# First unit of a fused attention and gated-FFN kernel: pair 0 by the hardware queue, key maxima from PSUM, turns ahead of scores

## The chip, the cores and the metric

The kernel runs on one core of one Trainium2 chip. The metric is the device time in microseconds (us) of one execution; lower is better. Executions of one kernel agree within about 0.8%, so differences of 1 us (0.4%) need several runs, and most experiments below were timed in five rounds against the kernel before on the same chip. PE is the matmul engine, DVE the vector engine, ACT the scalar engine, POOL the engine that issues the casting DMAs (the software queue), and SP the engine that issues the others (the hardware queue).

## The reference, cut to what matters

```python
# q, k, v: (4, 8, 768, 64); out: (3072, 512)
k_sum = k.reshape(B, H, 24, 32, D).max(axis=3)      # one key per block of 32: the maximum
v_sum = v.reshape(B, H, 24, 32, D).mean(axis=3)     # one value per block: the mean
# softmax over a band of +-15 positions and the 24 block keys together
a = softmax(concat([masked(q k^T / 8), q k_sum^T / 8 + log(32)]))
x = a @ concat([v, v_sum])                          # heads side by side: 512 wide
# gated FFN, 512 -> 1536 -> 512, on all 3072 rows
out = x + sigmoid(x @ w_res) * ((gelu(x @ w_gate) * (x @ w_val)) @ w_out)
```

The kernel cuts the work into eight units of half a sequence (384 rows). In a unit the eight heads are four pairs; a pair fills the 128 partitions of a transpose. A unit is: turn q and k (transpose), scores, exponential, attention, transpose of the output (`xp` to `xT`), gate and value matmuls in twelve output blocks (fo 0 to 11), and the second FFN matmul. The attention of unit n+1 is woven into the FFN of unit n, so only the attention of the first unit stands bare. That bare part, the prologue, is what the change works on.

## The kernel before

The parts that the change and the argument touch, with cuts marked:

```python
# PSUM: eight banks. mm has four buffers, s one of two banks, ao and t one bank each
MM, AO, TT, SS = (ps_mm, "mm"), (ps_o, "ao"), (ps_t, "t"), (ps_s, "s")
...
load_tokens(kt, k, 0, 0, S, 0, 4)          # all loads on POOL, float32 cast to bf16
select(ident[:], ALU.not_equal, 1.0, 0, -1, 1)
load_tokens(qa, q, 0, 0, TU, 0, 4)
load_tokens(kt, k, 0, 0, S, 4, 8)
load_tokens(qa, q, 0, 0, TU, 4, 8)
... # v in seven pieces, then the weights in column chunks, then q's second half
keep_warm(13, wp)                          # matmuls on zeros, nobody reads them
for hp in range(2):
    k_step(0, hp, *MM)
    q_step(qa, 0, 0, TU, hp, *MM)
... # mask and scores of pair 0, turns of pair 2, scores of pair 1, and so on
for c in range(3, NC + 1):                 # block means of v, a piece at a time
    vsum_sum(0, *MM, range(c, c + 1), vs)
    keep_warm(2 if c < NC else 1, wp)
vsum_out(0, vs, 0, 2, nc.vector.tensor_copy)
vsum_out(0, vs, 2, 8, nc.scalar.copy)
homes = (AO, TT, MM, MM)                   # PSUM of the attention outputs of the four pairs
for p in (0, 2):
    for hp in (p, p + 1):
        av_part(0, hp, st, *homes[hp], blocks=False)   # the band
    for hp in (p, p + 1):
        av_part(0, hp, st, blocks=True)                # the block values
        av_norm(hp, st)                                # two DVE operations
keep_warm(3)
...
for hp in range(NP):
    xt_step(0, hp, st, *(TT if hp % 2 else AO), nc.scalar.copy)   # PSUM of the transposes
    ... # gate and value matmuls of fo 0 and 1, a quarter of the depth at a time
```

The zero matmuls (`keep_warm`, 30 of them in the prologue) keep PE occupied. And the first transpose (pair 0) writes to the bank `AO`, which holds the attention output of pair 0: it may start when pair 0 has been normalised, which it needs anyway.

The softmax here doesn't subtract the row's maximum and nothing guards it: scores larger than these inputs give would overflow.

Of the kernel before, what the change touches and what calls it, by code (L numbers as in the profile page):

```python
# [15 lines left out]
def kernel(  # L16
# [86 lines left out]
    with tc.manual_schedule():  # L103
# [17 lines left out]
        def mask_consts():  # L121
            nc.vector.memset(maskt[:], 1.0)
            select(maskt[0:96], ALU.is_ge, 0.0, -1, -1, 1)
            select(maskt[0:96], ALU.is_ge, 0.0, 2 * WIN - 1, 1, -1)
            nc.vector.tensor_scalar(nmask[:], maskt[:], 30000.0, -30000.0, ALU.mult, ALU.add)

# [4 lines left out]
        nc.vector.memset(bmean[:], 1.0 / BLK)  # L131
        vext_consts(0)

        kt, qa, qb = token_tile(0, S, "k0"), token_tile(0, TU, "qa"), token_tile(TU, S, "qb")
        k_sb[0] = kt
        load_tokens(kt, k, 0, 0, S, 0, 4)
        select(ident[:], ALU.not_equal, 1.0, 0, -1, 1)
        load_tokens(qa, q, 0, 0, TU, 0, 4)
        load_tokens(kt, k, 0, 0, S, 4, 8)
        load_tokens(qa, q, 0, 0, TU, 4, 8)  # L140
        select(bias_t[96:128, :], ALU.is_ge, -30000.0, NB - 1, 0, -1)
        load_values(0, 0)
        mask_consts()
        kw_consts(0)
        load_values(0, 1)
        select(bmean[:], ALU.is_ge, 0.0, 32 * (NB + 94) - WIN, -32, 1)
        select(bmean[:], ALU.is_ge, 0.0, 31 + WIN - 32 * (NB + 94), 32, -1)
        for c in range(2, NC + 1):
            load_values(0, c)
        nc.vector.memset(vsum[0][96:128, :, D:D + 1], 1.0)  # L150
# [3 lines left out]
        for c in range(6):  # L154
            sl = slice(c * 256, (c + 1) * 256)
            nc.gpsimd.dma_start(out=w_gate[:, :, sl], in_=wg_src[:, :, sl])
            nc.gpsimd.dma_start(out=w_val[:, :, sl], in_=wv_src[:, :, sl])
        load_tokens(qb, q, 0, TU, S, 0, H)
# [55 lines left out]
        def q_step(src, b, lo, hi, hp, pool, tag):  # L214
            tp = turn_pair(src, hp, pool, tag)
            nc.scalar.copy(qT[b % 2][hp][:, lo:hi].rearrange("d (p j) -> d p j", j=tp.shape[2]), tp)
# [59 lines left out]
        def mask_step():  # L276
            s = ps_s.tile([128, 2, 512], F32, tag="s", name="s")
            for hh in range(2):
                nc.tensor.matmul(s[:, hh, 0:TU].rearrange("p (t q) -> p t q", t=HT), ident[:],
# [4 lines left out]
        def s_step(u, hp, st, s=None, two=None, masked=True):  # L284
            b, half = u // 2, u % 2
            first = s is not None
            if two:
# [129 lines left out]
        def values_step(u, fo):  # L417

            b = u // 2 + 1
            first = 8  # L420
            if u in (2, 4) and first - 3 <= fo < first + 1:
                block_sums(vT[b], fo - first + 3)
            if u in (1, 2, 4) and fo >= first:
# [11 lines left out]
                if i in (2, 3):  # L435
                    vsum_bc(nb, 2 * i - 4, 0, HT)
                    vsum_bc(nb, 2 * i - 3, 0, HT)
# [9 lines left out]
        wp = ps_o.tile([128, 512], F32, tag="ao", name="wp")  # L447
        keep_warm(13, wp)
        nc.scalar.activation(pre[:], bias_t[0:1, :], AF.Exp)
        for hp in range(2):  # L450
            k_step(0, hp, *MM)
            q_step(qa, 0, 0, TU, hp, *MM)
        s = mask_step()
        keep_warm(3, wp)
        s_step(0, 0, st, s)
        k_step(0, 2, *MM)
        q_step(qa, 0, 0, TU, 2, *MM)
        s = mask_step()
        s_step(0, 1, st, s)
        k_step(0, 3, *MM)  # L460
        q_step(qa, 0, 0, TU, 3, *MM)
        s = mask_step()
        s_step(0, 2, st, s)
        v_spread(0, 0, HT // 2, 0)
        v_spread(0, 0, HT // 2, 1)
        vs = vsum_sum(0, *MM, range(0, 3))
        keep_warm(2, wp)
        s = mask_step()
        s_step(0, 3, st, s)
        keep_warm(2, wp)  # L470
        for c in range(3, NC + 1):
            vsum_sum(0, *MM, range(c, c + 1), vs)
            keep_warm(2 if c < NC else 1, wp)
        vsum_out(0, vs, 0, 2, nc.vector.tensor_copy)
        vsum_out(0, vs, 2, 8, nc.scalar.copy)
        nc.scalar.activation(pre[:], bias_t[0:1, :], AF.Gelu)
        homes = (AO, TT, MM, MM)
        for p in (0, 2):
            for hp in (p, p + 1):
                av_part(0, hp, st, *homes[hp], blocks=False)  # L480
            for hp in (p, p + 1):
                av_part(0, hp, st, blocks=True)
                av_norm(hp, st)
        keep_warm(3)
# [7 lines left out]
        for u in range(NU):  # L492
# [17 lines left out]
            for fo in range(FO):  # L510
# [33 lines left out]
                if u == 0 and fo >= FO - 2:  # L544
                    for hp in range(2 * (fo - FO + 2), 2 * (fo - FO + 2) + 2):
                        q_step(qb, 0, TU, S, hp, *(TT if hp % 2 else AO))
# [108 lines left out]
```

## Time and profile before

| | |
|---|---|
| time, median of 3 runs | 265.32 us (264.82 to 265.44) |
| span of the profiled execution | 262.5 us |
| PE busy | 96% of the span |
| last block means of v that wait for a load | 18.17 us |
| first gate matmul | 23.24 us |
| gate matmuls without gaps | from 25.60 us |

The first lines of parts 1 and 2 of the page: busy time and share of each engine, and PE's busy tenths in 40 slices of the span with the granted clock.

```profile
PE 251.4 (96%) x2263; PEld 142.0 (54%) x2288; DVE 174.8 (67%) x414; ACT 133.2 (51%) x228; POOL 100.1 (38%) x136
...
PE   7799999999999999999899999999999999999994
...
PEclk9999999999999999999999999999999999999999
```

The reader sees that PE is short of work only in the first two slices of 6.6 us each. The chain of waits (the work that ended last, in order of time: start, length, what):

```profile
10.30 7.83 DMA vext<-in_v_dram
...
18.17 0.38 PE vs L254
18.55 0.43 PE wp L415 x2
18.98 0.32 PE vs L254
...
19.68 2.07 PE ao L328 x96
21.75 0.16 issue
21.91 0.59 PE wp L415 x2
22.51 0.18 PE xp L347 x3
```

The chain waits for v to land, then makes the block means (vs) with zero matmuls (wp) between them, the whole attention (ao), three more zero matmuls (the trace holds two of them), and the transposes (xp).

### The profile page before, as it was taken

The numbers are of one execution on the slowest core, as the hardware profiler recorded it, in microseconds if no ns is written. First come the engines' busy times: TensorE is split into PE (matmuls) and PEld (weight loads), VectorE is DVE, ScalarE is ACT, GpSimd is POOL, SyncE is SP. The second block draws the span as 40 slices with busy tenths as digits, with TensorE's granted clock in tenths as the row PEclk, the third lists the DMA queues.
The fourth block names the chain that finished last, engine by engine and source line by source line (L and its number), as shares of the span: only waits on it lengthen the run. The fifth ranks groups of instructions, "written<-read, shape, count | busy, mean of one in ns | idle before, by whom it ended". The sixth has DMA issues, their size and how long they took to land.

```text
span 262.5 us, 5776 instructions
## 1 busy us (share of the span) xinstructions
PE 251.4 (96%) x2263; PEld 142.0 (54%) x2288; DVE 174.8 (67%) x414; ACT 133.2 (51%) x228; POOL 100.1 (38%) x136
## 2 busy tenths in 40 slices
PE   7799999999999999999899999999999999999994
PEld 2536555556555565556455565455645565555543
DVE  3754862589385889877836799687739763674424
ACT  2745449557575535745274535734364536453310
POOL 7966642997799305998500200010000100020000
PEclk9999999999999999999999999999999999999999
DMA  5999999999999999999991785344002200130012
GB/s 78 175 168 196 197 205 192 144 153 191 106 117 121 205 147 109 147 174 194 136 72 32 175 151 96 16 104 125 0 4 75 93 0 2 30 124 13 1 40 82
DMA packets 113483, 28.83 MB, mean 110 GB/s; under 512 B 100400, under 2 KB 111280, under 8 KB 113456
## 3 DMA queue, kind: packets, MB, share of 16 engines
q0 software_dynamic: 86992, 19.41, 87.3%
q1 hardware_dynamic: 26464, 9.05, 18.1%
q8 instruction: 18, 0.29, 0.5%
q14 instruction: 9, 0.07, 0.1%
HBM read 32.51 MB, written 6.29 MB: 148 GB/s over the span
## 4 chain that ended last, share of the span: by engine, by line
PE 86%; DMA 6%; POOL 3%; issue 1%; DVE 1%; ACT 1%; POOLq 0%; DVEq 0%
PE f L398 23%; PE vv L364 21%; PE g L364 20%; PE r L382 8%; PE ao L328 4%; PE gv L508 3%; DMA vext<-in_v_dram 3%; DMA kW<-k_sb 3%; PE s L296 2%; POOL vext L99 2%; PE xp L347 1%; PE tp L185 1%; PE vs L254 1%; PE gv L364 1%; POOL k L90 1%
## 5 line engine op out<-in xcount | busy, mean ns | idle before, releaser
L364 PE MATMUL vv<-xT,w_val 128*128 128x384 bf16 x364 | 74.5, 326 | 0.0
L370 ACT ACTIVATE ge<-g 128x384 f32<-128x384 f32 x87 | 42.8, 492 | 59.5 <-PE g L364 33.9
L364 PE MATMUL g<-xT,w_gate 128*128 128x384 bf16 x348 | 71.3, 326 | 1.2 <-DVE gvT L371 1.2
L371 DVE TENSOR_TENSOR gvT<-ge,vv 128x384 bf16<-128x384 f32 x91 | 49.6, 551 | 27.9 <-PE vv L364 26.3
L398 PE MATMUL f<-w_out,gvT 128*128 128x512 bf16 (+2 forms) x298 | 66.6, 362 | 0.7
L364 PEld LDWEIGHTS <-w_val 128*128 128x128 bf16 x368 | 36.0, 98 | 24.5 <-issue 0.9
L364 PEld LDWEIGHTS <-w_gate 128*128 128x128 bf16 x352 | 33.8, 98 | 23.3 <-issue 1.8
L409 POOL DMA_DIRECT2D out_dram<-o x12 | 6.6, 546 | 98.8 <-DVE rz L336 83.9
L398 PEld LDWEIGHTS <-gvT 128*128 128x128 bf16 x312 | 28.3, 98 | 28.2
L388 ACT ACTIVATE th<-r 128x512 f32<-128x512 f32 x24 | 14.2, 602 | 25.8 <-PE r L382 25.8
L172 POOL DMA_DIRECT2D k_sb<-in_k_dram x24 | 20.1, 853 | 12.9 <-DMA w_out<-in_moe_w_out_dram 5.3
L403 DVE SCALAR_TENSOR_TENSOR th<-th,f 128x512 f32<-128x512 f32 (+2 forms) x26 | 16.7, 641 | 12.3 <-PE f L398 8.5
L382 PE MATMUL r<-w_res,xT 128*128 128x512 bf16 x88 | 23.7, 380 | 0.6 <-issue 0.3
L99 POOL DMA_DIRECT2D vext<-in_v_dram x28 | 23.2, 870 | 1.4 <-PE vv L364 0.8
L313 DVE TENSOR_TENSOR P<-P,maskt 128x768 bf16<-128x768 bf16 x28 | 15.5, 558 | 11.5 <-ACT P L305 7.5
L172 POOL DMA_DIRECT2D q_sb<-in_q_dram x24 | 19.7, 863 | 0.0
L338 DVE TENSOR_TENSOR xn<-ao,rz 128x384 bf16<-128x384 f32 x32 | 17.8, 557 | 1.1
L349 ACT COPY xT<-xp 128x384 bf16<-128x384 bf16 x20 | 9.3, 482 | 17.5 <-PE xp L347 17.5
L305 ACT ACTIVATE P<-s,bias_t 128x768 bf16<-128x768 f32 x18 | 16.3, 906 | 3.0 <-PE s L296 2.9
L405 DVE SCALAR_TENSOR_TENSOR o<-th,xn 128x512 f32<-128x512 f32 (+2 forms) x26 | 16.9, 651 | 0.9
L336 DVE RECIPROCAL rz<-ao 128x6 f32<-128x6 f32 x32 | 6.0, 189 | 13.1 <-PE ao L328 13.1
L302 ACT ACTIVATE P<-s,bias_t 128x384 bf16<-128x384 f32 x28 | 14.6, 578 | 0.0
(87 smaller groups left out, 247.2 us busy)
## 6 DMA issues: line engine op xcount, KB each, us to landing
out_dram<-o POOLq DMA_DIRECT2D x12, 256.0 KB, 2.8
out_dram<-o SPq DMA_DIRECT2D x11, 256.0 KB, 5.1
vext<-in_v_dram POOLq DMA_DIRECT2D x20, 128.0 KB, 7.3
k_sb<-in_k_dram POOLq DMA_DIRECT2D x24, 96.0 KB, 6.2
q_sb<-in_q_dram POOLq DMA_DIRECT2D x24, 96.0 KB, 4.1
w_gate<-in_moe_w_gate_dram POOLq DMA_DIRECT2D x6, 256.0 KB, 8.9
w_val<-in_moe_w_val_dram POOLq DMA_DIRECT2D x6, 256.0 KB, 9.1
w_out<-in_moe_w_out_dram POOLq DMA_DIRECT2D x3, 512.0 KB, 14.1
```

The source lines that it names most:

```text
L99: nc.gpsimd.dma_start(out=dst, in_=v[b, :, lo:hi, :].rearrange("h p d -> p h d"))
L172: nc.gpsimd.dma_start(out=sb[b][:, h // 2, :, h % 2 * D:h % 2 * D + D], in_=src[b, h].rearrange("(c p) d -> p c d", c=NC))
L305: nc.scalar.activation(P.rearrange("p a t q -> p a (t q)"), s[:, :, 0:TU], AF.Exp, scale=scale, bias=bias_t[:])
L313: nc.vector.tensor_mul(Pf, Pf, maskt.unsqueeze(1).to_broadcast([128, 2 * HT, QT]))
L338: nc.vector.tensor_mul(xn, ao[:, :, :, 0:D], rz.to_broadcast([128, NSUB, 2, D]))
L364: nc.tensor.matmul(acc[:, 0:TU], w[:, ko, fs], st["xT"][:, ko, :], start=(ko == 0), stop=(ko == KO - 1))
L370: nc.scalar.activation(ge[:], g[:, 0:TU], AF.Gelu)
L371: nc.vector.tensor_mul(gvT[:, fo, :], ge[:], vv[:, 0:TU])
L382: nc.tensor.matmul(r[:], st["xT"][:, ko, ss], w_res[:, ko, :], start=(ko == 0), stop=(ko == KO - 1))
L398: nc.tensor.matmul(st["f", sub][:, 0:c1 - c0], gvT[:, fo, ss], w_out[:, fo, c0:c1], start=(fo == 0), stop=(fo == FO - 1))
L403: nc.vector.scalar_tensor_tensor(th, th, 1.0, f[:, 0:c1 - c0], ALU.add, ALU.mult)
L405: nc.vector.scalar_tensor_tensor(o[:, 0:c1 - c0].rearrange("p (k d) -> p k d", d=128), th.rearrange("p (k d) -> p k d", d=128), 0.5, st["x ...
```

## The change

Its intent: start the first scores earlier, have the band part of the attention done before v has fully landed, and so reach the dense part sooner. Pair 0 of k and q comes by the hardware queue in float32 and is cast on ACT and DVE. The key maxima are reduced straight from the transposes in PSUM, and only for the half of the tiles that the first unit needs; the other half (`k_later`) is filled in amid the gate. Each pair's turns stand ahead of the scores of the pair before. q's second half is loaded ahead of the last weight chunk and turned behind fo 9.

```diff
-        load_tokens(kt, k, 0, 0, S, 0, 4)
+        nc.sync.dma_start(out=kf[:], in_=k[0, 0:2].rearrange("h (p j) d -> p h (j d)", j=8))
+        nc.sync.dma_start(out=qf[:], in_=q[0, 0:2, 0:TU].rearrange("h (p j) d -> p h (j d)", j=4))
+        load_tokens(kt, k, 0, 0, S, 2, 4)
         select(ident[:], ALU.not_equal, 1.0, 0, -1, 1)
-        load_tokens(qa, q, 0, 0, TU, 0, 4)
-        load_tokens(kt, k, 0, 0, S, 4, 8)
-        load_tokens(qa, q, 0, 0, TU, 4, 8)
+        load_tokens(qa, q, 0, 0, TU, 2, 4)
+        for h in (4, 6):
+            load_tokens(kt, k, 0, 0, S, h, h + 2)
+            load_tokens(qa, q, 0, 0, TU, h, h + 2)
+        select(maskt[0:96], ALU.is_ge, 0.0, -1, -1, 1)
+        select(maskt[0:96], ALU.is_ge, 0.0, 2 * WIN - 1, 1, -1)
+        load_values(0, 0)
... (cut: constants earlier; the block values of three later units moved to other output blocks; in the weight loop:)
+            if c == 5:
+                load_tokens(qb, q, 0, TU, S, 0, H)
... (cut: k_first, which copies a turned pair; its second half:)
+        def k_first_rest(tp, kw):
+            ks = work.tile([128, NB], BF16, tag="ks", name="ks")
+            nc.vector.tensor_reduce(out=ks[:], in_=tp.rearrange("d j (n w) -> d n j w", w=4),
+                                    axis=mybir.AxisListType.XY, op=ALU.max)
+            ... three copies for the first HT tiles; k_later makes the same three for the others
... (cut; the prologue, its end:)
-        keep_warm(13, wp)
+        keep_warm(8, s1[0])
...
-        homes = (AO, TT, MM, MM)
-        for p in (0, 2):
-            for hp in (p, p + 1):
-                av_part(0, hp, st, *homes[hp], blocks=False)
-            for hp in (p, p + 1):
-                av_part(0, hp, st, blocks=True)
-                av_norm(hp, st)
-        keep_warm(3)
+        homes = (MM, MM, AO, TT)
+        for hp in range(2):
+            av_part(0, hp, st, *homes[hp], blocks=False)
+        vsum_sum(0, *MM, range(4, 5), vs)
+        for hp in range(2, NP):
+            av_part(0, hp, st, *homes[hp], blocks=False)
+        keep_warm(1, wp)
+        vsum_sum(0, *MM, range(5, NC + 1), vs)
         vsum_out(0, vs, 0, 2, nc.vector.tensor_copy)
         vsum_out(0, vs, 2, 8, nc.scalar.copy)
+        for hp in range(NP):
+            av_part(0, hp, st, blocks=True)
+            av_norm(hp, st)
... (cut; in the gate loop of the first unit:)
-                if u == 0 and fo >= FO - 2:
-                    for hp in range(2 * (fo - FO + 2), 2 * (fo - FO + 2) + 2):
+                if u == 0 and 4 <= fo < 8:
+                    k_later(kW[0][fo - 4])
+                if u == 0 and fo == FO - 3:
+                    for hp in range(NP):
                         q_step(qb, 0, TU, S, hp, *(TT if hp % 2 else AO))
```

The homes of the attention outputs had to move, because the scores of pairs 1 and 3 now use the banks `AO` and `TT`.

More of the change, by code (lines that the diff above doesn't have):

```diff
@@ L119, in select @@
                                     pattern=[[step, ap.shape[-1]]], channel_multiplier=cm)
-        def mask_consts():
-            nc.vector.memset(maskt[:], 1.0)
-            select(maskt[0:96], ALU.is_ge, 0.0, -1, -1, 1)
-            select(maskt[0:96], ALU.is_ge, 0.0, 2 * WIN - 1, 1, -1)
-            nc.vector.tensor_scalar(nmask[:], maskt[:], 30000.0, -30000.0, ALU.mult, ALU.add)
         nc.vector.memset(warm[:], 0.0)
@@ L131 @@
         nc.vector.memset(bmean[:], 1.0 / BLK)
+        nc.vector.memset(maskt[:], 1.0)
         vext_consts(0)
+        kw_consts(0)
+        nc.vector.memset(vsum[0][96:128, :, D:D + 1], 1.0)
         kt, qa, qb = token_tile(0, S, "k0"), token_tile(0, TU, "qa"), token_tile(TU, S, "qb")
         k_sb[0] = kt
-        load_tokens(kt, k, 0, 0, S, 0, 4)
-        select(ident[:], ALU.not_equal, 1.0, 0, -1, 1)
-        load_tokens(qa, q, 0, 0, TU, 0, 4)
-        load_tokens(kt, k, 0, 0, S, 4, 8)
-        load_tokens(qa, q, 0, 0, TU, 4, 8)
+        kf = qk.tile([PP, 2, 8 * D], F32, tag="k_sb", name="kf")
+        qf = qk.tile([PP, 2, 4 * D], F32, tag="q_sb", name="qf")
+        nc.sync.dma_start(out=kf[:], in_=k[0, 0:2].rearrange("h (p j) d -> p h (j d)", j=8))
+        nc.sync.dma_start(out=qf[:], in_=q[0, 0:2, 0:TU].rearrange("h (p j) d -> p h (j d)", j=4))
+        load_tokens(kt, k, 0, 0, S, 2, 4)
+        select(ident[:], ALU.not_equal, 1.0, 0, -1, 1)
+        load_tokens(qa, q, 0, 0, TU, 2, 4)
[5 more added lines that the diff above has]
+        load_values(0, 0)
         select(bias_t[96:128, :], ALU.is_ge, -30000.0, NB - 1, 0, -1)
-        load_values(0, 0)
-        mask_consts()
-        kw_consts(0)
-        load_values(0, 1)
+        for c in range(1, NC + 1):
+            load_values(0, c)
         select(bmean[:], ALU.is_ge, 0.0, 32 * (NB + 94) - WIN, -32, 1)
         select(bmean[:], ALU.is_ge, 0.0, 31 + WIN - 32 * (NB + 94), 32, -1)
-        for c in range(2, NC + 1):
-            load_values(0, c)
-        nc.vector.memset(vsum[0][96:128, :, D:D + 1], 1.0)
         wg_src = moe_w_gate.rearrange("(ko ki) f -> ki ko f", ki=128)
@@ L155 @@
             sl = slice(c * 256, (c + 1) * 256)
+            if c == 5:
+                load_tokens(qb, q, 0, TU, S, 0, H)
             nc.gpsimd.dma_start(out=w_gate[:, :, sl], in_=wg_src[:, :, sl])
             nc.gpsimd.dma_start(out=w_val[:, :, sl], in_=wv_src[:, :, sl])
-        load_tokens(qb, q, 0, TU, S, 0, H)
         nc.gpsimd.dma_start(out=w_res[:], in_=moe_w_res.rearrange("(ko ki) f -> ki ko f", ki=128))
@@ L212, in k_rest, with q_step, k_first, k_later @@
             nc.vector.tensor_copy(kw[:, :, BLK0:BLK0 + NB], ks.unsqueeze(1).to_broadcast([128, NT, NB]))
-        def q_step(src, b, lo, hi, hp, pool, tag):
+        def q_step(src, b, lo, hi, hp, pool, tag, copy=nc.scalar.copy):
             tp = turn_pair(src, hp, pool, tag)
-            nc.scalar.copy(qT[b % 2][hp][:, lo:hi].rearrange("d (p j) -> d p j", j=tp.shape[2]), tp)
+            copy(qT[b % 2][hp][:, lo:hi].rearrange("d (p j) -> d p j", j=tp.shape[2]), tp)
+        def k_first(hp):
+            tp = ps_mm.tile([128, 8, PP], BF16, tag="mm", name="tp")
+            for j in range(8):
+                for hh in range(2):
+                    nc.tensor.transpose(tp[hh * 64:hh * 64 + 64, j, :], kt[:, 2 * hp + hh, j, :], ident[0:PP, 0:PP])
+            kw = kW[0][hp]
+            nc.scalar.copy(kw[:, :, OWN:OWN + QT].rearrange("d t (p j) -> d t p j", j=8),
+                           tp.rearrange("d j (t p) -> d t p j", t=NT))
+            return tp, kw
+        def k_first_rest(tp, kw):
+            ks = work.tile([128, NB], BF16, tag="ks", name="ks")
+            nc.vector.tensor_reduce(out=ks[:], in_=tp.rearrange("d j (n w) -> d n j w", w=4),
+                                    axis=mybir.AxisListType.XY, op=ALU.max)
+            nc.vector.tensor_copy(kw[:, 0:HT, BLK0:BLK0 + NB], ks.unsqueeze(1).to_broadcast([128, HT, NB]))
+            nc.vector.tensor_copy(kw[:, 1:HT, 0:WIN], kw[:, 0:HT - 1, OWN + QT - WIN:OWN + QT])
+            nc.vector.tensor_copy(kw[:, 0:HT, POST:POST + WIN], kw[:, 1:HT + 1, OWN:OWN + WIN])
+        def k_later(kw):
+            nc.vector.tensor_copy(kw[:, HT:NT, 0:WIN], kw[:, HT - 1:NT - 1, OWN + QT - WIN:OWN + QT])
+            nc.vector.tensor_copy(kw[:, HT:NT - 1, POST:POST + WIN], kw[:, HT + 1:NT, OWN:OWN + WIN])
+            nc.vector.tensor_copy(kw[:, HT:NT, BLK0:BLK0 + NB], kw[:, 0:HT, BLK0:BLK0 + NB])
         def turn_batch(b, p0, p1):
@@ L274, in vsum_bc, with s_tiles, mask_into @@
             nc.vector.tensor_copy(vext[b % 2][96:128, lo:hi, 2 * hp:2 * hp + 2, 0:D], src)
-        def mask_step():
-            s = ps_s.tile([128, 2, 512], F32, tag="s", name="s")
+        def s_tiles(two=None):
+            if two:
+                return [pool.tile([128, 512], F32, tag=tag, name="s1") for pool, tag in two]
+            return ps_s.tile([128, 2, 512], F32, tag="s", name="s")
+        def mask_into(s):
+            two = isinstance(s, list)
             for hh in range(2):
-                nc.tensor.matmul(s[:, hh, 0:TU].rearrange("p (t q) -> p t q", t=HT), ident[:],
+                nc.tensor.matmul((s[hh] if two else s[:, hh])[:, 0:TU].rearrange("p (t q) -> p t q", t=HT), ident[:],
                                  nmask.unsqueeze(1).to_broadcast([128, HT, QT]),
@@ L286, in s_step @@
             first = s is not None
-            if two:
+            if two and not first:
                 s = [pool.tile([128, 512], F32, tag=tag, name="s1") for pool, tag in two]
@@ L419, in values_step @@
             b = u // 2 + 1
-            first = 8
+            first = 9 if u == 1 else 8
             if u in (2, 4) and first - 3 <= fo < first + 1:
@@ L434, in values_step @@
                     v_spread(nb, 0, HT // 2, 1)
-                if i in (2, 3):
-                    vsum_bc(nb, 2 * i - 4, 0, HT)
-                    vsum_bc(nb, 2 * i - 3, 0, HT)
+                for hp in range(NP):
+                    if (i, u) in (((hp + 2) // 2, 1), ((hp + 4) // 2, 2), ((hp + 4) // 2, 4)):
+                        vsum_bc(nb, hp, 0, HT)
             if u % 2 == 0 and u < NU - 1:
@@ L446 @@
         st = new_unit()
-        wp = ps_o.tile([128, 512], F32, tag="ao", name="wp")
-        keep_warm(13, wp)
         nc.scalar.activation(pre[:], bias_t[0:1, :], AF.Exp)
-        for hp in range(2):
-            k_step(0, hp, *MM)
-            q_step(qa, 0, 0, TU, hp, *MM)
-        s = mask_step()
-        keep_warm(3, wp)
+        s1 = s_tiles((AO, TT))
+        keep_warm(8, s1[0])
+        nc.scalar.copy(kt[:, 0].rearrange("p j d -> p (j d)"), kf[:, 0])
+        nc.vector.tensor_copy(kt[:, 1].rearrange("p j d -> p (j d)"), kf[:, 1])
@@ L455 @@
+        nc.vector.tensor_copy(qa[:, 0:2].rearrange("p h j d -> p h (j d)"), qf[:])
+        t = k_first(0)
+        q_step(qa, 0, 0, TU, 0, *MM, nc.vector.tensor_copy)
+        nc.vector.tensor_scalar(nmask[:], maskt[:], 30000.0, -30000.0, ALU.mult, ALU.add)
+        k_first_rest(*t)
+        t = k_first(1)
+        q_step(qa, 0, 0, TU, 1, *MM)
+        k_first_rest(*t)
+        s = mask_into(s_tiles())
+        keep_warm(2, s1[0])
         s_step(0, 0, st, s)
-        k_step(0, 2, *MM)
+        keep_warm(2, s1[0])
@@ L457 @@
+        mask_into(s1)
+        t = k_first(2)
         q_step(qa, 0, 0, TU, 2, *MM)
-        s = mask_step()
-        s_step(0, 1, st, s)
-        k_step(0, 3, *MM)
-        q_step(qa, 0, 0, TU, 3, *MM)
-        s = mask_step()
-        s_step(0, 2, st, s)
+        k_first_rest(*t)
+        s_step(0, 1, st, s1, True)
+        s = mask_into(s_tiles())
+        t = k_first(3)
+        q_step(qa, 0, 0, TU, 3, *MM, nc.vector.tensor_copy)
+        k_first_rest(*t)
+        vs = ps_mm.tile([128, DM], F32, tag="mm", name="vs")
@@ L464 @@
+        keep_warm(1, vs)
+        s_step(0, 2, st, s)
+        s3 = mask_into(s_tiles((AO, TT)))
+        wp = ps_mm.tile([128, 512], F32, tag="mm", name="wp")
+        vsum_sum(0, *MM, range(0, 2), vs)
+        keep_warm(2, wp)
+        s_step(0, 3, st, s3, True)
+        nc.scalar.activation(pre[:], bias_t[0:1, :], AF.Gelu)
         v_spread(0, 0, HT // 2, 0)
         v_spread(0, 0, HT // 2, 1)
-        vs = vsum_sum(0, *MM, range(0, 3))
+        vsum_sum(0, *MM, range(2, 4), vs)
         keep_warm(2, wp)
-        s = mask_step()
@@ L469 @@
-        s_step(0, 3, st, s)
-        keep_warm(2, wp)
-        for c in range(3, NC + 1):
-            vsum_sum(0, *MM, range(c, c + 1), vs)
-            keep_warm(2 if c < NC else 1, wp)
+        homes = (MM, MM, AO, TT)
[6 more added lines that the diff above has]
+        vsum_sum(0, *MM, range(5, NC + 1), vs)
@@ L474 @@
         vsum_out(0, vs, 0, 2, nc.vector.tensor_copy)
         vsum_out(0, vs, 2, 8, nc.scalar.copy)
-        nc.scalar.activation(pre[:], bias_t[0:1, :], AF.Gelu)
-        homes = (AO, TT, MM, MM)
-        for p in (0, 2):
-            for hp in (p, p + 1):
-                av_part(0, hp, st, *homes[hp], blocks=False)
-            for hp in (p, p + 1):
-                av_part(0, hp, st, blocks=True)
-                av_norm(hp, st)
-        keep_warm(3)
+        for hp in range(NP):
+            av_part(0, hp, st, blocks=True)
+            av_norm(hp, st)
@@ L543 @@
                         k_step(nb, hp, *home)
-                if u == 0 and fo >= FO - 2:
-                    for hp in range(2 * (fo - FO + 2), 2 * (fo - FO + 2) + 2):
+                if u == 0 and 4 <= fo < 8:
+                    k_later(kW[0][fo - 4])
+                if u == 0 and fo == FO - 3:
+                    for hp in range(NP):
                         q_step(qb, 0, TU, S, hp, *(TT if hp % 2 else AO))
```

## The prediction

> **What bounds the kernel now.** The page gives a span of 262.5 us, PE busy 96%; the chain of waits is 86% PE: from 25.6 us on PE runs almost without a gap. Only the prologue has slack. The timeline shows the first gate matmul at 23.24 us, gate and value matmuls dense only from 25.60 us. In the chain the prologue is the pool's DMA issues to 10.3 us, 7.83 us of DMA landing of v (until 18.13), two block-mean matmuls with keep-warm matmuls between (to 19.6), 96 attention matmuls (2.07), keep-warm matmuls (0.6), then transposes, ACT copies and gate. So the landing of v, call it L = 18.1 us, and the tail behind it (7.5 us to dense gate) decide; the scores are done earlier (last exponential ends 16.66).
>
> **What the change does.**
> 1. Pair 0 of k and q goes by the hardware queue in float32 and is cast on ACT and DVE. The DMA view shows 49 to 74 GB/s until 4.5 us; the hardware queue can use that hole. The Trainium skill (DMA: Bandwidth & Descriptors, Issuing engines are not separate DMA queues) says that both queues share 16 engines, so it is no new bandwidth; it takes 295 KB (of 1.97 MB before v has landed) from the pool's stream, 1.5 us at the 200 GB/s of the trace. v is issued later (estimate 6.6 instead of 4.76 us), but there is a backlog: v took 6 to 7.8 us to land. I expect L near 16.4 us, and the first transposes near 5.3 us instead of 6.55.
> 2. Key maxima from PSUM: one reduction (estimate 0.85 us) replaces 0.36 + 0.55; the shifts are halved. With the next pair's turns ahead, ACT limits the scores: casts, copies and exponentials of about 9 us from 4.3 us on. Last exponential estimated 15.4 us, so v still ends last.
> 3. The band part of the attention moves ahead of L; after L remain two block-mean matmuls, their copies (0.3), 48 short matmuls, four normalisations of 0.7 us on DVE, transposes and copies. First gate at L + 2.7, dense gate at L + 5.1 = about 21.5 us instead of 25.6. Expected gain there 4.1 us.
> 4. Given back: the weights follow v in the same queue, so they move by about 1.5 us only, while PE asks 4 us earlier; before, each 256 KB piece landed about 3 us ahead of its use (pool waits 21.86 to 33.96). q's second half now goes ahead of the last piece, 2 us more for it. Expect small PE waits on w_gate/w_val, above all at fo 10, 0.3 to 0.6 us. k_later puts 12 copies (some 1.6 us) into fo 4 to 7, where DVE also sets 2 us of constants and PE already waited on gvT: 0.3 us.
>
> Later stages keep their order; only a DMA landing at 128.5 us (keys, 7.65 us in the chain) could swallow some of it.
>
> **Prediction:** 265.3 - 4.1 + 0.8 = 262.0 us; 8 in 10 between 260.3 and 263.8. Faster by over 2% (under 260.0): 0.09; within 2%: 0.90; slower: 0.01.
>
> **What would show it.** Timeline: first PE transpose near 5.3; last block-mean matmuls near 16.4; first gate near 19.1; dense gate near 21.5; PE waits on weights at fo 10; from dense gate to the end under 1 us longer than before (237 us).
>
> **What would make it wrong.** v not landing earlier, because its packets of 128 B or its later issue limit it (then 263.5). The scores ending last: ACT's casts, or nmask, which waits for the pool's mask selects behind six loads (then 263). Or weights landing well ahead and L near 15.5 (then 260.5).

## The result, and the profile after

The changed kernel took 266.21 us (median of 4 runs, 266.0 to 266.5) against 265.07 us (4 runs). The ratio is 1.0045, with a 95% interval of 1.0022 to 1.0067. Ratios in this document are the mean time of one kernel's fast runs over that of the other's in the same rounds, so they are not quite the ratio of the medians quoted. A gain of 3.3 us was forecast and a loss of about 1 us came: the change is within 2%, as forecast, but on the other side of zero and outside the range.

The same lines of the page after:

```profile
PE 251.0 (95%) x2251; PEld 141.3 (53%) x2276; DVE 176.1 (67%) x426; ACT 133.4 (50%) x229; POOL 101.3 (38%) x138
...
PE   7977999999999999999899999999999999999993
...
PEclk9997999999999999999999999999999999999999
```

PE's busy time is the same, but the third and fourth slices have a busy tenth of 7, and in the fourth the granted clock falls. The chain of waits after:

```profile
9.88 6.78 DMA vext<-in_v_dram
...
16.70 0.38 PE vs L280
17.08 0.50 PE ao L359 x24
17.58 0.16 issue
17.74 0.72 PE vs L280 x2
...
19.48 0.56 DVE xn L369
...
20.17 0.56 DVE xn L369
...
20.87 0.56 DVE xn L369
...
21.56 0.57 DVE xn L369
22.13 0.05 issue
22.17 0.50 PE xp L378 x3
22.67 0.64 PE gv L395 x2
```

The chain now waits for an earlier piece of v: 16.65 is the landing of the fifth of the seven pieces (17.21 before), 18.13 was that of the sixth. The last two pieces landed at 17.52 and 17.74, before the change at 18.13 and 18.29, so v is about 0.6 us earlier. The attention behind it is shorter. But now all four normalisations (xn) stand in the chain one after another, and the transposes come behind the last of them. The timeline of PE (start, length, engine, line, operation, output and inputs, form, and in brackets how long the engine had been idle and what released it) shows what the first transposes waited for:

```profile
18.83 1.27 PE L359 MATMUL ao<-vsum,P 32*64 32x65 bf16 x48 [0.39 <-DVE vsum L285]
21.48 0.34 PE L378 MATMUL xp<-ident,xn 128*128 128x128 bf16 x3 [1.38 <-DVE xn L369]
22.17 0.50 PE L378 MATMUL xp<-ident,xn 128*128 128x128 bf16 x3 [0.35 <-DVE xn L369]
22.46 0.53 PE L395 MATMUL gv<-xT,w_gate 128*128 128x384 bf16 x1
22.79 0.53 PE L395 MATMUL gv<-xT,w_val 128*128 128x384 bf16 x1
```

The first three transposes are those of pair 0, whose own normalisation ended at 20.04 (in the chain, 19.48 + 0.56). They start at 21.48, when the third normalisation, that of pair 2, has ended (in the chain, 20.87 + 0.56 = 21.43). Before the change the same step read, in the same view:

```profile
22.34 0.50 PE L347 MATMUL xp<-ident,xn 128*128 128x128 bf16 x6
23.24 0.32 PE L364 MATMUL gv<-xT,w_gate 128*128 128x384 bf16 x1 [0.40 <-ACT xT L349]
23.40 0.32 PE L364 MATMUL gv<-xT,w_val 128*128 128x384 bf16 x1
```

A gate matmul takes 0.53 us after the change and 0.32 before, and they start 0.32 apart instead of 0.16. The windows view (stretch, its length, busy time and count of PE, weight loads, DVE, ACT and POOL, then granted clock, DMA share and GB/s) gives the clock; before:

```profile
20.00:22.00 2.00, 1.84 (x89) 1.71 (x84) 1.33 (x5) 1.63 (x3) 1.52 (x3) 1.00 1.45 197
22.00:23.00 1.00, 0.84 (x8) 0.49 (x8) 0.93 (x5) 0.29 (x1) 0.60 (x1) 1.00 1.46 196
```

and after:

```profile
20.00:22.00 2.00, 0.44 (x10) 0.17 (x3) 1.90 (x7) 0.14 (x1) 1.56 (x3) 1.00 1.43 196
22.00:23.00 1.00, 0.83 (x5) 0.60 (x6) 0.12 (x1) 0.62 (x2) 0.00 (x0) 0.58 1.46 192
23.00:24.00 1.00, 1.00 (x6) 0.56 (x5) 0.00 (x0) 0.19 (x1) 0.76 (x1) 0.50 1.45 195
24.00:25.00 1.00, 1.00 (x6) 0.52 (x5) 0.00 (x0) 0.48 (x1) 0.74 (x1) 0.50 1.44 195
25.00:26.00 1.00, 1.00 (x8) 0.68 (x7) 0.00 (x0) 0.18 (x1) 0.53 (x1) 0.72 1.46 198
```

From 20 to 22 us PE was busy for 0.44 us of 2, and then ran at half clock for 3.4 us (22.15 to 25.56 by the clock record in the trace).

Put together, by the starts of the same instructions in the two timelines:

| stage | before | after | difference |
|---|---|---|---|
| last block means that waited for v | 18.17 | 17.74 | -0.43 |
| from there to dense gate (last quarter of fo 0) | 7.43 (to 25.60) | 8.61 (to 26.35) | +1.18 |
| from there to the first score matmul of the second unit | 15.15 (to 40.75) | 16.30 (to 42.65) | +1.15 |
| from there to the end of the span | 221.75 | 221.65 | -0.10 |
| span | 262.5 | 264.3 | +1.8 |

(The profiled execution of after is 1.8 us longer by its span and 1.4 by its time, 266.00 against 264.59; the medians differ by 1.1.) The third and fourth rows meet at the first score, and this point misleads a little: before the change the scores stop half-way for a copy. Counted to the first residual matmul behind them (41.87 and 43.11), only 0.49 of the 1.15 is lost. From there to the last matmul it is 0.11 more, and 0.48 lies behind the last matmul, a stretch that took between 3.6 and 4.8 us in the traces, so this last part may be chance. The loss that the change explains sits in the tail of the prologue and in the gate loop of the first unit, and next to nothing is lost in the seven other units.

### The profile page after: what moved, and what is told of

Read it like the earlier page. It is cut to its first block, busy times and chain, and to the rows that moved or that the text cites. A ratio compares the mean times of both kernels' runs of the same rounds, so it can differ in the third digit from the quotient of the medians.

```text
span 264.3 us, 5773 instructions
## 1 busy us (share of the span) xinstructions
PE 251.0 (95%) x2251; PEld 141.3 (53%) x2276; DVE 176.1 (67%) x426; ACT 133.4 (50%) x229; POOL 101.3 (38%) x138
## 4 chain that ended last, share of the span: by engine, by line
PE 82%; DMA 5%; DVE 5%; POOL 3%; issue 2%; ACT 0%; POOLq 0%; DVEq 0%
PE f L429 23%; PE vv L395 19%; PE g L395 19%; PE r L413 8%; PE ao L359 3%; PE gv L553 3%; DMA kW<-k_sb 3%; DMA vext<-in_v_dram 3%; PE s L327 2%; PE xp L378 1%; POOL vext L99 1%; DVE gvT L402 1%; PE vs L280 1%; PE tp L186 1%; DVE xn L369 1%
## 5 line engine op out<-in xcount | busy, mean ns | idle before, releaser
L395 PEld LDWEIGHTS <-w_val 128*128 128x128 bf16 x368 | 36.2, 98 | 24.6 <-issue 1.1
L344 DVE TENSOR_TENSOR P<-P,maskt 128x768 bf16<-128x768 bf16 x28 | 15.5, 557 | 10.2 <-ACT P L336 6.2
L173 POOL DMA_DIRECT2D q_sb<-in_q_dram x24 | 19.7, 853 | 1.2 <-DMA k_sb<-in_k_dram 1.2
L333 ACT ACTIVATE P<-s,bias_t 128x384 bf16<-128x384 f32 x32 | 16.7, 578 | 1.3 <-PE s L327 1.3
L336 ACT ACTIVATE P<-s,bias_t 128x768 bf16<-128x768 f32 x16 | 14.4, 903 | 2.1 <-PE s L327 2.0
```

The costliest lines, as they stand in the source:

```text
L173: nc.gpsimd.dma_start(out=sb[b][:, h // 2, :, h % 2 * D:h % 2 * D + D], in_=src[b, h].rearrange("(c p) d -> p c d", c=NC))
L333: nc.scalar.activation(P[:, hh].rearrange("p t q -> p (t q)"), s[hh][:, 0:TU], AF.Exp, scale=scale, bias=bias_t[:])
L344: nc.vector.tensor_mul(Pf, Pf, maskt.unsqueeze(1).to_broadcast([128, 2 * HT, QT]))
L395: nc.tensor.matmul(acc[:, 0:TU], w[:, ko, fs], st["xT"][:, ko, :], start=(ko == 0), stop=(ko == KO - 1))
```

## The experiments

All outputs are right. The theories at the start: H, the transposes' PSUM homes hold them back; C, the clock falls because PE has too little to do; D, the late key copies on DVE hold the gate back; T, four turns of q in one place hold it back. The rival to H and C was that four normalisations of 0.7 us in a row are simply the limit.

### Homes of the transposes

In the changed kernel pair 2's attention output lives in `AO` and pair 3's in `TT`, and the transposes of pairs 0 and 1 write to just these banks. The edit, on the changed kernel, gives them the four-buffer pool instead:

```diff
-            xt_step(0, hp, st, *(TT if hp % 2 else AO), nc.scalar.copy)
+            xt_step(0, hp, st, *homes[hp], nc.scalar.copy)
```

> The changed kernel, with one edit: the first two of the four transposes of the attention output (pairs 0 and 1) write their PSUM tile to the four-buffer pool instead of to the two single-buffer pools. Theory H (PSUM homes): in the changed kernel the transposes of pair 0 waited 1.4 us, until 21.48, for the normalisation of pair 2, because pair 2's attention output now sits in the bank they write to. Then they start near 20.1 us, the idle gap shrinks, the clock stays at 1.00, the third output block's gate starts near 23.5 instead of 27.0, and the time falls by about 3.2 us to about 263.0. If the gap is closed but the clock still falls to one half: about 264.7. Rival (the four normalisations of 0.7 us on DVE in a row are the limit whatever the homes): no change, 266.2.

Measured: 264.66 us (6 runs), ratio to before 0.9991 (0.9966 to 1.0016), so 1.5 us under the changed kernel's 266.21 (a comparison across two sets of rounds; against the kernel before in its own rounds, the changed kernel stood at 1.0045). The timeline of PE:

```profile
20.11 0.34 PE L378 MATMUL xp<-ident,xn 128*128 128x128 bf16 x3
20.80 0.34 PE L378 MATMUL xp<-ident,xn 128*128 128x128 bf16 x3 [0.35 <-DVE xn L369]
```

The 1.38 us wait is gone. From the last block means (17.76) to dense gate (24.97) are 7.21 us instead of 8.61, so 1.40 less. H holds and its rival falls. The clock still fell, from 21.4 to 24.9 us: the "if the gap is closed but the clock still falls" branch of the expectation. In two of the six executions the mean clock was 1.00; they took 263.77 and 264.67, so the 263.0 forecast for that case was not reached.

### Zero matmuls in the gap

```diff
             av_norm(hp, st)
+        keep_warm(6, wp)
```

> The changed kernel, with one edit: six keep-warm matmuls after the last attention matmuls, where PE had stood idle 1.4 us; the transposes' homes stay as in the change. Theory C (clock): the granted clock fell to one half from about 22.4 to 25.5 us because PE did too little from 20 to 22 us; with the fillers it stays at 1.00, the first transposes still start near 21.5 us, and the time falls by about 1.6 us to 264.6. Rival (the clock falls for another reason, or the fillers only delay): 266.2 or more.

Measured: 265.25 us, ratio 1.0011 (0.9988 to 1.0034), 1.0 us under the changed kernel. The mean granted clock of a whole execution shows how often it fell: 3.4 us at half clock in 264 make 0.994 (3.4 x 0.5 / 264 = 0.006). Here five of six executions had 0.996 or more; all four of the changed kernel had 0.993 or 0.994. So the fillers do hold the clock in most executions (these five average 265.1, 1.1 us under the changed kernel and not the 1.6 forecast). But the profiled execution is the sixth, and in it the clock fell at 19.7 us, ahead of the fillers. So the idle gap from 20 to 21.5 is not the whole cause: the stretch ahead of it, with short matmuls and small waits, can be enough. C holds, its mechanism wider than I had put it; what the traces say of it stands behind the last experiment.

### Late key copies behind later blocks

```diff
-                if u == 0 and 4 <= fo < 8:
-                    k_later(kW[0][fo - 4])
+                if u == 0 and fo >= 8:
+                    k_later(kW[0][fo - 8])
```

> The changed kernel, with one edit: the twelve late key copies on DVE are made behind output blocks 8 to 11 instead of 4 to 7. Theory D: they lengthened DVE's backlog behind the constants of block 4 and cost PE about 0.4 us at blocks 8 and 9; the step from block 8 to block 9 falls from 1.79 us to 1.4 and the time by 0.4 us to 265.8. Rival (the constants alone make the backlog, as before the change): no change.

Measured: 266.53 us, ratio 1.0063 (1.0038 to 1.0088): no gain in the time. In the profile the gate loop did get shorter. From the gelu of fo 2 in unit 0 to the same one in unit 1 it took 31.79 us instead of 32.37 (before the change: 31.89), and from fo 8 to fo 9 1.40 instead of 1.79. But the prologue of this execution was 1.4 us longer. Its zero matmuls and transposes ran at half pace until 10.5 us instead of 5.1, so the first scores came late, and the clock fell once more from 24.2 to 27.6 us. Three of the six executions had a mean clock of 0.987 to 0.989, which is more than one fall. D is right about the stage (0.58 us, which covers the loss of the gate loop up to the first residual matmul, 0.49), and the total hides it: by the late start in the profiled execution, by the clock in three others.

### Turns of q two pairs at a time

```diff
-                if u == 0 and fo == FO - 3:
-                    for hp in range(NP):
+                if u == 0 and fo >= FO - 2:
+                    for hp in range(2 * (fo - FO + 2), 2 * (fo - FO + 2) + 2):
```

> The changed kernel, with one edit: q's second half is turned two pairs each behind blocks 10 and 11, as before the change, not four pairs behind block 9; it is still loaded early. Theory T: four turns through two PSUM banks waited for ACT's copies; PE's gap of 0.4 us goes and the time falls by about 0.6 us to 265.6. Rival: no change.

Measured: 267.34 us, ratio 1.0093 (1.0065 to 1.0122). The wait of 0.4 us on ACT's copies is gone from its place, and the stretch to the first score matmul is 0.56 us shorter (26.80 to 41.89, against 27.00 to 42.65). But the scores then stop half-way for ACT's copy of the turns that have just been made, as they did before the change, and by the next residual matmul nothing is left: 16.21 us from fo 2, against 16.11 in the changed kernel. T falls: the change had only moved this wait. The higher total is not explained: three of the six executions lie at 266.3 to 266.9 and three at 267.8 to 267.9, all with a clock of 0.992 to 0.994, so the second group has a loss that the mean granted clock doesn't show. The profiled execution (266.27) is of the first group. A late first warm-up as in the run before would fit, for it left the mean clock at 0.994 too, but it isn't shown.

### Homes, late copies and turns together

> The changed kernel with three edits at once: the homes of the first two transposes (H), the late key copies behind blocks 8 to 11 (D), q's second half turned two pairs at a time (T). If the three stage gains seen one by one add up (1.4 us before the gate; 0.58 and 0.56 us in the gate loop), the gate loop from the third block to the first score of the next unit takes 14.5 us as before the change (15.65 in the changed kernel), and the time is about 263.7, that is 1.0 us under the kernel before. Rival: the gate loop then meets the weights, and part of the gain becomes PE waits on w_gate or w_val.

Measured: 264.0 us against 264.91 (11 runs), ratio 0.9967 (0.9948 to 0.9987): faster than the kernel before. In its profiled execution the clock stayed at 1.00 from the first warm-up to the end of the work, and from the last block means to dense gate it reads:

```profile
18.17 0.70 PE L280 MATMUL vs<-vext,bmean 128*128 128x512 bf16 x2 [0.16 <-issue]
...
23.79 0.32 PE L395 MATMUL gv<-xT,w_gate 128*128 128x384 bf16 x1
```

These are 5.62 us, where the homes alone gave 7.21: the half clock had cost 1.59 us. The gate loop from fo 2 to the first score takes 14.39 us (24.44 to 38.83), as expected, and PE waits for no weights. The gain of this execution at the first unit, 1.9 us, is still there at the last unit (1.84); so no later unit swallows it. Behind the last matmul this execution then took 4.65 us where the one before took 3.60, so that the spans differ by 0.8 and the times by 1.2 (263.38 against 264.59).

### Thirteen more zero matmuls

The run before, plus `keep_warm` in PE's gaps: 2 between the first turns, 2 and 3 more ahead of the third and fourth scores, 1 or 2 at three places around the block means, 2 behind them, 1 between two transposes.

> The run before with keep-warm matmuls put into PE's gaps between 5.8 and 20.8 us (13 more). Theory C (the change took keep-warm matmuls away, 30 before and 18 after, so that a window of low PE activity halves the clock): the clock stays at 1.00 from 10 to 27 us in all or nearly all runs, third gate block at 24.0 instead of 25.6 us, and the time is about 1.6 us less than that run, about 262.1. Rival (the fillers delay the work, or the clock falls all the same): as that run.

Measured: 263.45 us, ratio 0.9952 (0.9929 to 0.9976). All six executions have a clock of 0.997 or more, so it held. But the gain is 0.5 us and not 1.6. In the runs compared, only two of six had fallen, and the fillers cost time themselves: in the profiled executions fo 2 starts at 25.18 us instead of 24.44.

### Delayed issue of v

Step 1 of the prediction had v landing 1.7 us earlier. It landed 0.6 us earlier, and the block means came 0.4 us earlier. Is the issue to blame, which moved from 4.76 to 6.24 us? The edit on the changed kernel (one look, not timed in rounds):

```diff
+        for _ in range(4):
+            select(scr[:], ALU.not_equal, 1.0, 0, -1, 1)     # idle work on POOL
         load_values(0, 0)
```

> The changed kernel with 1.2 us of idle work (four selects of 0.3 us on a scratch tile) on the pool just ahead of the first load of v; the bytes stay the same. Theory I (the landing of v follows the pool's issue, which the change moved from 4.76 to 6.24 us): the last block-mean matmuls, at 17.74 us, come 1.2 us later, near 18.9. Rival B (the bytes in the DMA engines decide): they stay within 0.4 us of 17.7.

The DMA packets of the trace answer it. v's 6,144 packets of 128 B, by the time at which a share of them had ended, and the first packet of any load:

```
                        first load   50% of v   98% of v   last of v
before                       2.92      12.59      15.53      17.30
changed                      1.86      11.83      14.65      16.39
changed, issue + 1.2 us      1.86      12.90      15.64      16.52
changed, pair 1 too          1.86      12.66      16.06      16.65
```

The delay moved the bulk by 1.0 us but the last packet by only 0.13. Theory I falls: what ends last does not follow the issue. The last two pieces landed at 17.49 and 17.68, as in the changed kernel (17.52 and 17.74). The last 2% of the packets (a DMA engine's sixteenth would be 6%) trail the rest by about 1.75 us in both kernels. The last block means came at 18.10 instead of 17.74, just within the rival's range, and not for v: PE waited 1.32 us for the constant of the block means, which POOL makes behind the loads, and the first of them came at 14.31 instead of 12.99.

The last column varies by itself. In nine traces whose loads are those of the changed kernel, v's last packet ended between 16.01 and 16.83 us (mean 16.34), and in two with the loads of the kernel before at 17.30 and 16.81. So this one look shows that the end did not move by 1.2 us, and no more than that.

### The kernel before with fewer zero matmuls

18 instead of 30: 8 in front, 2 instead of 3 ahead of the first scores, 1 behind each block mean, none ahead of the transposes.

> The kernel before, with its keep-warm matmuls cut from 30 to 18, the count of the changed kernel (8 in front, and the three ahead of the output transposes taken out); nothing else. Theory C: the clock now falls to one half for about 3.4 us somewhere before 27 us in most runs, or the first warm-up comes later in some, and the time rises by about 1.6 us to 266.3 in those. Rival (the count does not matter): 264.7, or a little faster, since PE does less.

Measured: 263.59 us, ratio 0.998 (0.9942 to 1.0018), and two groups. Four executions took 263.3 to 263.7 (clock 0.991 to 0.997), about 1.4 us less than before: the zero matmuls stood in the chain. The two others took 265.15 and 266.94, with a clock of 0.977 and 0.979. In the profiled one of them the clock is half from 8.5 to 15.3 and from 22.2 to 25.6 us. So in the old kernel too the smaller count lets the clock fall, in some executions; and the part of the expectation that called for a slower kernel in most runs was wrong. Zero matmuls are a trade: they cost time when the clock would have held.

### Five more zero matmuls, and seven

The run with three edits, with five more where its timeline shows PE idle; then two more between the first turns:

```diff
-        keep_warm(1, vs)
+        keep_warm(3, vs)
...
-        keep_warm(2, wp)
+        keep_warm(4, wp)
         s_step(0, 3, st, s3, True)
...
             xt_step(0, hp, st, *homes[hp], nc.scalar.copy)
+            if hp == 0:
+                keep_warm(1, wp)
```

> The run with the three edits, with five more keep-warm matmuls only where PE stands idle by its timeline (2 more ahead of the third score step, 2 more ahead of the fourth, 1 between the first two output transposes). Theory C: as with thirteen more, the clock holds in nearly all runs, but without the 0.7 us that those cost ahead of the last attention part; time about 263.2, clock at 0.997 or more but for the tail. Rival (five are not enough to hold the clock): as the run with three edits, 264.0, with some runs at 0.994 or less.

> As the run with five more, and two more keep-warm matmuls between the transposes of pairs 0 and 1, near 5.9 us. Theory C2 (with 8 instead of 13 matmuls in front, PE warms up late in some executions, up to about 10 us, which costs about 1.5 us and does not show in the granted clock of a run): the slow tail of the distribution (runs 1.5 us above the fastest at clock 1.00) goes. Rival: the same spread of 1.5 to 2 us remains.

With five: 263.06 us against 264.4, ratio 0.9943 (0.9912 to 0.9974), the lowest of all, though not clear of the 0.9952 with thirteen, and faster than the kernel before. Four executions took 262.8 to 263.07 at a clock of 1.00. Two took 264.4 and 265.01 at 0.994 and 0.987, and the second of these is the profiled one (falls at 7.6 to 11.0 and at 21.2 to 24.6 us). With seven: 264.33 us, ratio 0.9987 (0.9959 to 1.0014). The spread did shrink, 264.2 to 264.9 without the one slow execution, but to a level 1.3 us higher. Its profiled execution was slow (clock 0.944), so nothing is read from it.

> The same kernel as the run with five more and two in front, for a profile in the fast state: its runs were 264.2 to 264.9 at a granted clock near 1.00, 1.3 us over the fastest without the two in front, and its profiled execution fell in a slow state. Theory W: the two matmuls run at half pace and push the first scores back by 0.6 to 1 us, which the chain to the last attention part passes on; the first score step then starts near 9 us instead of 8.3, or the third gate block near 25.5 instead of 24.4. Rival: the prologue is as without them, and the 1.3 us is lost later (a stage behind the first unit).

Measured: 264.44 us (2 runs), ratio 0.9996 (0.9954 to 1.0038). The first score step starts at 8.36 us and fo 2 at 25.04, so the two matmuls do not delay the scores, and theory W falls in its first mark; the second (25.5) can't be judged, since in this execution the clock was half from 19.7 to 23.2 us. 0.55 us more was lost between the sixth and the seventh unit. Why the seven are worse than the five stays open; a comparison of so few executions in a quantity that depends on how the clock's monitor happens to stand is thin.

### Pair 1 by the hardware queue too

> The changed kernel, with pair 1 of k and q also by the hardware queue in float32 and cast on ACT and DVE; 295 KB less in the pool's queue, and 1.3 us less of pool issue. Theory S (the last 2% of v's packets lag because one part of the software queue is backlogged by bytes since the start): as pair 0 brought the last packet from 17.30 to 16.39, pair 1 brings it to about 15.5. Rival (its end is set by something else, as under the delayed issue where it moved 0.13 us): it stays at 16.2 to 16.6. No gain in time expected in either case, for ACT and DVE have 2 us more to cast.

Measured: 270.76 us (one run). The last packet of v ended at 16.65 us; it did not move to 15.5, and theory S falls, as far as one execution of unknown state can show it. The hardware queue's loads, with twice the bytes on it, ended at 9.5 us instead of 4.2, so the turns of pair 1 started at 9.3 us, and with the waiting the clock fell twice.

What the four rows of packets above have in common: the bytes to be read ahead of v's end are the same in all of them, whatever queue they are on, and only the start differs. The first packet of any load came 1.07 us earlier after the change (1.86 instead of 2.92), and the last of v 0.91 us earlier in this pair of traces, or 0.7 by the means given above. That would fit DMA engines, or one slow one among them, that are busy from first to last packet. It is not shown: no run moved the start alone, and the trace does not name the engine of a packet. The Trainium skill says in "DMA: Bandwidth & Descriptors", section "Issuing engines are not separate DMA queues", that loads from all engines run on the same 16 DMA engines and interleave; these runs agree, with 4.2 us becoming 9.5.

How often the clock fell, over timed executions whose clock was listed (0.994 or less counts as a fall; a fall behind the last matmul also counts, so this is an upper bound):

```
changed, changed + late copies moved, changed + turns moved   16 of 16
changed + homes                                                4 of 6
changed + six zero matmuls                                     1 of 6
homes, copies and turns together                               2 of 6
the same + 13 zero matmuls                                     0 of 6
the same + 5                                                   2 of 6
the same + 7 (its slow execution left out)                     2 of 7
before                                                         4 of 36
before with 18 zero matmuls                                    4 of 6
```

In the times a fall is worth 0.7 to 1.8 us: among the executions of one kernel those with a fall were slower in the mean by 0.7 (homes), 0.9 (homes, copies and turns) and 1.8 us (the same + 5), with two to four executions on each side. A mean clock alone doesn't tell it, though: with 18 zero matmuls the kernel before had two executions at 0.991 and 0.992 that cost nothing (263.73 and 263.33).

What decides a fall? The experiments looked at idle gaps; the kept traces say something else. Their clock records change only at steps of 3.41 us, so each such window at full clock can be set beside what followed it. The array share below is an estimate: of each matmul the part of the 128x128 array that it fills (rows x columns, as the timeline gives them: 96*64 and 32*64 for the attention, 128*128 for gate and zero matmuls) times its moving columns (384 in 0.16 us, as the gate matmuls show), over the window.

```
trace, window                      PE busy  longest idle  array share  then
before            18.42 to 21.84     96%      0.06 us        0.32      held
before, 18 zero   18.76 to 22.17     95%      0.11           0.34      fell
changed           18.74 to 22.15     43%      1.38           0.09      fell
delayed issue     11.82 to 15.23     48%      1.32           0.33      held
six zero matmuls  16.24 to 19.66     80%      0.39           0.27      fell
three edits       16.33 to 19.74     81%      0.39           0.29      held
+ 13              18.10 to 21.51     96%      0.07           0.45      held
```

Busy time and gaps do not part the falls from the others. The array share does so but for a narrow band: of the windows that began at full clock up to 250 us in 13 traces (the slow one left out), all seven below 0.285 were followed by a fall, none of the 889 above 0.37, and between the two six fell and six held. So a stretch of attention or transposes can drop the clock while PE hardly stands idle, and a zero matmul would count for so much because it fills the whole array. This is read from the traces afterwards; no run varied the array share alone.

## Why the prediction was wrong

The prediction said 262.0 us, by a gain of 4.1 us in the prologue and 0.8 us given back. Measured against its steps:

- **Step 3, "First gate at L + 2.7, dense gate at L + 5.1": this step failed.** The sum had every operation in it but not the places where they write. Its first gate at L + 2.7 leaves no room for the transposes of pair 0 to wait for more than pair 0. The diff swaps the homes, so they wait for pair 2; the first gate came 4.72 us behind the last block means, and 3.26 behind them with the homes undone. The tail from the last block means to dense gate measured 8.61 us. Of the excess of 3.5 us over the 5.1 forecast, the homes are 1.40 (undone by one line, measured), the half clock is 1.59 (the difference between an execution with and one without it), and 0.5 remains as plain mis-sizing. With both out of the way the tail was 5.62 us, so the list of operations was about right.
- **The clock was in no step.** The prediction left the removed zero matmuls out of its tail, as pure gain. They were that in part (four executions of the old kernel with fewer gained about 1.4 us), but the changed kernel fell to half clock in every execution listed. The Trainium skill gives a rule in "TensorE: Matmul & The Clock Gate", section "Why this matters for your kernels": no idle gaps of more than about 3 us. By that rule alone a gap of 1.4 us is safe. In this trace the clock fell with a longest gap of 1.38 us; here the measurement decides. The same page's section "What's actually happening" gives a window of 3.4 us and a half rate, and that agrees: half from 22.15 to 25.56 us.
- **Step 1, "L near 16.4": wrong in size.** The mechanism that both queues share the engines was named and then not used. 295 KB were counted as leaving the queue ahead of v, worth 1.5 us, though the same engines had to move them. v's last pieces landed 0.6 us earlier, and not 1.7; that the earlier start of all loads is the reason is likely but not shown. Of the 0.61 of the sixth piece (17.52 instead of 18.13), 0.43 reached the block means, since the band attention (until 17.58) and one zero matmul, which the trace lacks, stand in PE's order ahead of them.
- **Step 2, the scores: right in kind.** The reduction from PSUM took 0.95 us (estimate 0.85) in place of 0.36 + 0.55, so it removes no work. It removes no wait either, though it reads PSUM: in the trace it waits for ACT's copy of the same tile, and for pairs 1 to 3 it starts 0.03 us behind that copy's end (7.87, 10.83 and 12.85), as the first operation on the keys did before the change (7.95 behind 7.92). The first transposes came at 4.87 us (forecast 5.3). The last exponential ended at 16.0 us (forecast 15.4) and v still decided, but only by 0.2 us, the wait ahead of the block means of the fifth piece.
- **Step 4, given back.** No PE wait on weights appeared; the forecast of 0.3 to 0.6 us was wrong. The late key copies cost 0.5 to 0.6 us (forecast 0.3). Besides them no further cost was found: the turns of q moved a wait without changing its size.
- **"Later stages keep their order": right.** From the first residual matmul to the last matmul, 217.11 us against 217.00.

So the sum reads: forecast dense gate at 21.5 us; 1.3 us for v, 1.40 for the homes, 1.59 for the clock and 0.5 for the rest make 26.3; measured 26.35.

## What to carry to other kernels

When a change reorders work through a fixed set of PSUM banks, write down for each bank who leaves and who enters: a first-needed result that enters the bank of a last-finished one waits for it, however short both are, and one edited line decides it. Before counting zero matmuls or other filler as waste, look for stretches of small matmuls, which fill little of the array, and ask what the clock does there without the filler; and judge such a change by many executions with their clocks, since one profile can show either case. A load moved to another queue still uses the same DMA engines: count what they still have to move ahead of the load that is waited for, not what leaves its queue.

## What the Trainium skill lacked or had wrong

- "TensorE: Matmul & The Clock Gate" (section "Why this matters for your kernels") advises against idle gaps over about 3 us. As a sufficient rule it fails here: the clock fell to one half behind windows with no gap over 1.38 us (the three profiled ones of the 16 executions without fillers and without the homes edit; by the mean clock all 16 fell), at a cost of 1.59 us in the tail, and behind one with none over 0.11 us. The page's section "A second HAM failure mode: psum-queue depth-cycling" does name frequent short idle times as another cause; with a longest gap of 0.11 us and PE 95% busy, that doesn't cover this case either.
- No page says that a matmul seems to count for the clock by the part of the array that it fills: windows under an estimated share of 0.285 fell in 7 of 7 cases, windows over 0.37 in 0 of 889.
- "TensorE: Matmul & The Clock Gate" (section "Why this matters for your kernels") asks for 4 us of continuous work for the first warm-up. The 8 zero matmuls in front lasted 3.3 to 3.6 us. In 12 of 13 traces that was enough (full clock from 4.1 to 6.3 us), in one PE ran at half pace until 10.5 us, at a cost of 1.4 us. What the page lacks is how this looks in a profile: the granted clock of the windows view read 1.00 in that stretch, because the clock record begins only at 10.55 us, and the durations (0.63 us instead of 0.38 for a zero matmul) are the sign.
- "DMA: Bandwidth & Descriptors" names two engines that are usually slower (section "Latency and other measured facts") but gives no size for what that does to a load's landing: here the last 2% of v's packets trail the others by about 1.75 us in both kernels, and a delay of 1.2 us in the issue moved the last packet by 0.13 us. Whether those are the engines it names, no run here shows.
